# New queue orders and engine choices ahead of the first gate groups of a transformer block

## The chip, the cores and the metric

The kernel runs on one core of a Trainium2 chip. What is measured is the device time in microseconds. A core has five engines, each with an instruction queue that is worked off in order: TensorE (PE, with its weight loads shown apart as PEld), VectorE (DVE), ScalarE (ACT), GpSimd (POOL) and SyncE (SP), which here only issues DMA transfers. An instruction that must wait for a semaphore holds up all that stands behind it on its engine.

## What is computed

One block of a transformer in bfloat16, with 2048 rows (S) and width 448 (D): linear attention with 16 heads of 28 over feature maps, and a gated MLP of width 1792 (F).

```
x  = A_x                                      # 1 x 2048 x 448
q, k, v = split(layernorm(x) @ wqkv)          # 16 heads of 28
phi(t) = concat(softmax(t @ w_phi), softmax(-t @ w_phi))
kv = sum over s of phi(k)[s] v[s];   z = sum over s of phi(k)[s]
o  = (phi(q) @ kv) / (phi(q) . z + 1e-6)
h  = x + o @ wo
g, u = layernorm(h) @ w_gate, layernorm(h) @ w_up
out = h + (sigmoid(g) * u) @ w_down
```

## The kernel before

The rows are cut into 16 tiles of 128 rows, t = 0 to 15. The program builds a graph of about a thousand named operations with their data dependences; class `Graph` (L19 on) keeps them. Nothing orders them at run time but the table `ORDER` (from L209), which lists for each of the five queues the names in the order in which they are issued. Where an operation may run on one of two or three engines, its tuple of engines is given with it, and it goes to the engine in whose list its name stands (`Graph.op`). `emit` sets a semaphore wait wherever an operation needs another engine's result, or would overwrite what another still reads. So a name's place in the lists decides both the engine and the time.

The names, in order of the work:

- Loads on SP: `x0`, `x1` (one tile each), `x2`, `x4` ... `x14` (two tiles each); `ld_k0`, `ld_k2`, `ld_v0`, `ld_v2` (weights of k and v), `ld_q0` to `ld_q3` (weights of q, by transposing DMA), `ld_wo*`, `ld_wg*`, `ld_wu*`, `ld_wd0` to `ld_wd6` (output, gate, up and down weights). `wphi*` are small loads that ACT issues.
- First layernorm of tile t: `bst` and `agg` (mean and variance, DVE, L499 and L500), `ve1` (adds epsilon, L507), `pow1` (power -0.5, POOL only, L512), `nm1` (minus the mean, L510), `nb1` (bias, POOL only, L516), then `xn` (the normalized tile, L525 on ACT, L528 on DVE or POOL). `ve1`, `pow1`, `nm1`, `nb1` come by groups: tiles 0, 1, 2, 3 alone, then 4 and 5, 6 and 7, 8 to 11, 12 to 15; the number in the name is the first tile. Tiles 0 and 1 need no `nb1`; every other `xn` waits for the `nb1` of its group, whatever its engine.
- `xT`: transposes the normalized tile; for t < 4 on PE, with a copy `xTe` out of PSUM on ACT or DVE (`evac`, L485), else by a transposing DMA on SP (L538).
- Folding the feature map into the weights of k: `wT` (PE) and `wTe` (copy), `w2m0` (PE, L567) and `w2e0` (copy); `w2m1` and `w2e1` for q.
- k and v of a tile: `pp` and `vv` for pairs of the tiles 0 to 3, `pva`/`pvb` for the others (PE); `v1` copies v; `ek` takes two exponentials (ACT, L614 and L615), `ss` sums them (DVE, L618), `rs` inverts the sums (DVE, L619), `phi` multiplies (POOL or DVE, L622). `kva`/`kvb` add the tile to the running k/v sum in PSUM banks 6 and 7. There are 3 buffers for `phi`, 5 for `ek` and 5 for `v1`.
- `kvzones`, `kvzA` to `kvzD`: the masked copy of the k/v sum, with a column of ones (L426 to L429, L683, L687). They wait for `kvb15`.
- q by chunks of four tiles: `pqa`/`pqb` (PE), `eq` (two exponentials, ACT, L652 and L653).
- Attention output of a tile: `num` (PE), `rsm`, `qq`, `b`, `c`, `den`, `rden` (DVE, L714 to L725), `o` (POOL or DVE, L729), `oT` (transposed), `woa`/`wob` (PE).
- Residual and second layernorm: `h` (ACT for tiles 0 and 1, L748, else DVE, L751), `nm`, `sq` (ACT, L756), `ve` and `pow2` (POOL, L759 and L761), `hn` (DVE, L765), `hT`.
- MLP: gate groups `ga`/`gb` with tile and column group (PE), `sig` (ACT, L824), `hh` (DVE, L825), `dn`/`dp`/`dm`/`dl` (down projection, PE), `fin` (DVE), `out` (store).

`warm` are matmuls on zeros. Nearly all matmuls are recorded on line 296, that of the helper `both`, which issues two half-height matmuls side by side.

Of the kernel before, what the change touches and what calls it, by code (L numbers as in the profile page):

```python
# [925 lines left out]
```

## Time and profile before

| what | us |
|---|---|
| median of 3 runs | 205.27 (205.26 to 205.29) |
| span of the profiled execution, first to last instruction | 203.7 |
| busy PE | 196.7 (97%) |
| busy DVE | 135.9 (67%) |
| busy ACT | 97.4 (48%) |
| busy POOL | 57.9 (28%) |
| first gate matmul starts | 61.0 |

The span is that of one profiled execution; the time of a run lies 1.6 us above it. Busy matmul time is not time at full rate, as matmuls are pipelined. A row of the timeline gives start, length, engine, line, operation, the names of what it writes and reads, and in brackets the idle time before it with what ended it; rows of one kind that follow each other are merged (x3).

### The profile page before, as it was taken

How to read it: one execution, taken by the hardware profiler on the slowest of the kernel's cores; microseconds unless marked ns; L12 is line 12 of the kernel's file. 1: busy time of each engine (PE TensorE's matmuls, PEld its weight loads, DVE VectorE, ACT ScalarE, POOL GpSimd, SP SyncE). 2: the span in 40 equal slices, each digit the busy share in tenths (PEclk: the TensorE clock that was granted, in tenths of full speed). 3: DMA queues.
4: the chain of work that ended last, by engine and by line, in shares of the span. 5: the costliest groups of instructions: out<-in, count | busy, mean ns of one | idle time of the engine just before them, and what ended most of it. 6: DMA issues, size and time to landing. Idle time of an engine off the chain costs nothing.

```text
span 203.7 us, 5834 instructions
## 1 busy us (share of the span) xinstructions
PE 196.7 (97%) x2474; PEld 111.6 (55%) x2474; DVE 135.9 (67%) x340; ACT 97.4 (48%) x195; POOL 57.9 (28%) x98
## 2 busy tenths in 40 slices
...
GB/s 163 306 139 122 77 73 66 282 295 352 141 52 55 55 100 27 55 81 0 3 0 80 119 30 28 2 77 24 56 36 60 3 0 3 0 0 138 0 0 90
DMA packets 32866, 16.25 MB, mean 80 GB/s; under 512 B 25096, under 2 KB 31944, under 8 KB 32840
## 3 DMA queue, kind: packets, MB, share of 16 engines
...
q8 instruction: 19, 0.31, 0.7%
q10 hardware_dynamic: 504, 0.03, 0.2%
...
## 4 chain that ended last, share of the span: by engine, by line
PE 89%; DVE 4%; ACT 3%; DMA 1%; issue 1%; POOL 0%; DVEq 0%
PE psum L296 82%; PE psum L852 5%; DVE st L499 2%; DMA x_sb<-in_A_x_dram 1%; ACT eq L653 1%; ACT eq L652 1%; PE psum L567 1%; ACT junk L756 1%; ACT x_sb L748 1%; PE psum L492 1%; DVE kvz L683 1%; DVE mv L500 0%; DVE b_sb L717 0%; DVE c_sb L720 0%; POOL rst L512 0%
## 5 line engine op out<-in xcount | busy, mean ns | idle before, releaser
L296 PE MATMUL psum<-xnT,wg_sb 64*128 64x512 bf16 (+1 forms) x490 | 93.3, 333 | 0.4 <-ACT eq L653 0.2
L296 PE MATMUL psum<-xnT,wu_sb 64*128 64x512 bf16 (+1 forms) x490 | 93.0, 333 | 0.0
L824 ACT ACTIVATE sg_sb<-psum 128x512 bf16<-128x512 f32 (+1 forms) x70 | 35.0, 512 | 89.6 <-PE psum L296 89.0
L825 DVE SCALAR_TENSOR_TENSOR hhT<-sg_sb,psum 128x512 bf16<-128x512 bf16 (+1 forms) x70 | 39.0, 577 | 52.5 <-ACT sg_sb L824 52.1
L296 PEld LDWEIGHTS psum<-xnT,wg_sb 64*128 64x128 bf16 x490 | 44.3, 94 | 22.9 <-DVE hhT L825 4.8
L296 PEld LDWEIGHTS psum<-xnT,wu_sb 64*128 64x128 bf16 x490 | 44.3, 94 | 13.0
L296 PE MATMUL psum<-wd_sb,hhT 64*128 64x448 bf16 x336 | 36.9, 349 | 0.0
L296 PEld LDWEIGHTS psum<-wd_sb,hhT 64*128 64x128 bf16 x336 | 17.3, 94 | 14.8 <-DVE x_sb L751 0.6
L622 POOL TENSOR_TENSOR phi<-hhT,rs 128x896 bf16<-128x896 bf16 x14 | 24.1, 1738 | 0.9 <-PE psum L296 0.8
L296 PE MATMUL psum<-Wk,xnT 64*128 64x448 bf16 x112 | 22.3, 350 | 0.2
L296 PE MATMUL psum<-wv_sb,xnT 64*128 64x448 bf16 x112 | 22.4, 351 | 0.1
L759 POOL TENSOR_SCALAR ve<-ssq 128x1 f32<-128x1 f32 x16 | 3.1, 192 | 66.1 <-ACT junk L756 65.7
L618 DVE TENSOR_REDUCE ss<-hhT 128x32 f32<-128x896 bf16 x16 | 17.0, 1062 | 0.7 <-ACT hhT L615 0.7
L296 PE MATMUL psum<-xnT,Wq 64*120 64x512 bf16 x112 | 15.0, 385 | 0.1
L729 POOL TENSOR_TENSOR o_pad<-c_sb,rden 128x448 bf16<-128x448 bf16 x10 | 9.3, 936 | 15.6 <-DVE rden L725 13.4
L296 PE MATMUL psum<-wo_o,oT 64*128 64x448 bf16 x56 | 13.2, 350 | 0.0
L296 PE MATMUL psum<-wo_e,oT 64*128 64x448 bf16 x56 | 13.1, 349 | 0.0
L756 ACT ACTIVATE junk<-x_sb,nm 128x448 bf16<-128x448 bf16 x16 | 10.6, 661 | 1.9 <-DVE nm L754 1.8
L852 PE MATMUL psum<-wd_sb,hhT 128*128 128x448 bf16 (+2 forms) x70 | 11.1, 316 | 0.0
L859 DVE SCALAR_TENSOR_TENSOR x_sb<-psum,x_sb 128x448 bf16<-128x448 f32 (+2 forms) x17 | 9.4, 591 | 2.1 <-PE psum L852 1.6
L499 DVE BATCH_NORM_STATS2 st<-x_sb 128x6 f32<-128x448 bf16 x16 | 9.4, 611 | 1.9 <-DMA x_sb<-in_A_x_dram 1.9
L296 PEld LDWEIGHTS psum<-Wk,xnT 64*128 64x128 bf16 x112 | 7.6, 94 | 5.3 <-ACT hhT L615 0.7
...
## 6 DMA issues: line engine op xcount, KB each, us to landing
...
```

The costliest lines, as they stand in the source:

```text
L296: p = e.matmul(o, lhsT=w, rhs=r, start=st, stop=sp, tile_position=(row, 0))
L492: p = e.transpose(ps[:, kt * P:(kt + 1) * P], src, ident[:])
L499: op("dve", "bst%d" % t, lambda e: e.bn_stats(st1[:, t, :], x_sb[:, t, :]), r=[("x", t)], w=[("st1", t)])
L618: op("dve", "ss%d" % t, lambda e: e.tensor_reduce(ss[:, s, :], eks, AX.X, ALU.add), r=[("ek", s)], w=[("ss", s)])
L622: return e.tensor_tensor(phi[:, sp, :, :, :].rearrange("p b a n -> p (b a) n")[:, :, 0:56].rearrange("p b (h d) -> p b h d", h=2), eks.rea ...
L729: return e.tensor_tensor(o_pad[:, t % NO, off:off + D].rearrange("p (h d) -> p h d", h=H), c_sb[:, t % NS, :, 0:DH], rden[:, t % NS, :][:, ...
L756: op("act", "sq%d" % t, lambda e: e.activation(junk[:, t % 2, :], h_sb[:, t, :], ACT.Square, bias=nm2[:, t:t + 1], accum_out=ssq2[:, t:t + ...
L759: op("pool", "ve%d" % t, lambda e: e.tensor_scalar(ve2[:, t:t + 1], ssq2[:, t:t + 1], 1.0 / D, EPS, op0=ALU.mult, op1=ALU.add), r=[("ssq2" ...
L824: op("act", "sig" + nm, lambda e: e.activation(sg_sb[:, k, 0:N], bk(bg)[:, 0:N], ACT.Tanh, scale=0.5), r=[B(bg)], w=[("sg", k)])
L825: op("dve", "hh" + nm, lambda e: e.scalar_tensor_tensor(out=hhT[(t0 // 4) % NHH][:, ff, ns], in0=sg_sb[:, k, 0:N], scalar=1.0, in1=bk(bu)[ ...
L852: p = e.matmul(bk(b)[:, lo:hi], lhsT=hb[:, ff, TS(t)], rhs=wd_sb[:, ff, lo:hi], start=ff == 0, stop=ff == FT - 1)
L859: op("dve", "fin%d%s" % (t, nm), lambda e: e.scalar_tensor_tensor(out=h_sb[:, t, lo:hi], in0=bk(b)[:, lo:hi], scalar=0.5, in1=h_sb[:, t, l ...
```

## The change

Only the table `ORDER` changes; what each operation does, its buffers and its dependences stay. All five lists are new up to about the operations of the first gate group (tiles 0 and 1) and the same behind it. 38 operations change their engine:

- from ACT to DVE: `wTe0`, `wTe1`, `wTe2`, `xT0e`, `xT1e`, `xn4`, `xn13`, `xn15`, `w2e1_3`, `kvzones`
- from ACT to POOL: `xn6`, `xn11`, `xn14`
- from DVE to ACT: `wTe3`, `xT2e`, `v1_9`, `v1_10`; from POOL to ACT: `xn2`
- from DVE to POOL: `ve1_1`, `nm1_0`, `xn0`, `xn1`, `nm1_6`, `nm1_8`, `ve1_12`
- from POOL to DVE: `nm1_1`, `nm1_2`, `nm1_3`, `nm1_4`, `nm1_12`, `ve1_0`, `ve1_2`, `ve1_3`, `ve1_4`, `ve1_6`, `ve1_8`, `o2`, `o6`, `o7`

```diff
     "sp": (
-        "x1 x0 ld_k0 x2 ld_k2 x4 x6 ld_v0 x10 ld_v2 x8 ld_q2 ld_q1 ld_q0 x12 ld_q3 xT4 xT5 x14 xT6 xT7 xT8 xT9 xT10 "
-        "xT11 xT12 xT13 xT14 xT15 ld_wg0 ld_wu1 ld_wu3 ld_wd1 ld_wg1 ld_woe0 ld_wu0 ld_woe1 ld_woo0 ld_woo1 ld_wg3 "
-        "ld_wg2 ld_wd6 ld_wd2 ld_wd3 ld_wd5 ld_wd0 ld_wu2 oT2 oT3 oT5 oT4 oT6 oT7 ld_wd4 hT3 hT2 oT8 oT9 hT4 hT5 hT6 "
...
+        "x1 x0 x2 ld_k0 ld_k2 x4 x6 x10 ld_v2 x8 ld_v0 ld_wd4 ld_q2 x12 ld_q3 ld_q0 x14 ld_q1 xT4 ld_wg1 xT6 xT5 "
+        "xT7 xT8 xT9 xT10 xT11 ld_wg2 ld_wu3 xT12 ld_woo1 xT13 ld_wu0 xT14 xT15 ld_wu1 ld_woe0 ld_woe1 ld_wd2 "
+        "ld_wd0 ld_wg0 ld_wd5 ld_wu2 ld_wg3 ld_woo0 oT2 oT3 oT5 ld_wd1 oT4 oT6 oT7 hT3 ld_wd3 hT2 ld_wd6 oT8 oT9 "
...
     ),
     "act": (
-        "wphi3 wphi2 wphi1 wphi0 wTe0 wTe1 xT1e xT0e wTe2 w2e0_0 w2e0_1 w2e0_2 w2e0_3 xn3 xn4 ek0 ek1 xn5 v1_0 v1_1 "
-        "xn6 ek2 v1_2 v1_3 ek3 w2e1_1 ek4 v1_4 ek5 v1_5 w2e1_0 v1_6 ek6 xn11 ek7 v1_7 xn12 ek8 xn13 ek9 w2e1_3 w2e1_2 "
-        "ek10 xn14 ek11 xn15 v1_11 ek12 eq0_0 ek13 v1_13 ek14 v1_14 ek15 kvzones v1_15 eq0_1 kvzB eq1_0 eq1_1 eq2_0 "
-        "oT0e eq2_1 h1 h0 sq1 sq0 eq3_0 eq3_1 sig0_1 sig0_0 sig0_3 sig0_2 sig0_5 sig0_4 sq2 sig0_7 sig0_6 sq3 sig0_9 "
-        "sig0_8 sq5 sig0_11 sig0_10 sig0_13 sig0_12 sig2_1 sig2_0 sq4 sig2_3 sig2_2 sq7 sq6 sig2_5 sig2_4 sig2_6 "
...
+        "wphi0 wphi2 wphi1 wphi3 w2e0_0 wTe3 w2e0_1 w2e0_2 w2e0_3 xn2 xn3 xT2e ek0 ek1 v1_0 v1_1 xn5 ek2 v1_2 v1_3 "
+        "ek3 w2e1_0 ek4 v1_4 v1_5 ek5 w2e1_1 v1_6 ek6 ek7 v1_7 ek8 xn12 ek9 v1_9 w2e1_2 ek10 v1_10 ek11 v1_11 ek12 "
+        "eq0_0 ek13 v1_13 ek14 v1_14 ek15 v1_15 eq0_1 kvzB eq1_0 eq1_1 eq2_0 oT0e eq2_1 h1 h0 sq1 sq0 eq3_0 eq3_1 "
+        "sig0_1 sig0_0 sig0_3 sig0_2 sig0_5 sig0_4 sig0_7 sig0_6 sq2 sq3 sig0_9 sig0_8 sig0_11 sig0_10 sig0_13 "
+        "sig0_12 sq5 sig2_1 sig2_0 sq4 sig2_3 sig2_2 sq7 sq6 sig2_5 sig2_4 sig2_6 sig2_7 sig2_8 sig2_9 sig2_10 "
...
     ),
     "pe": (
-        "warm0 warm1 warm2 wT0 wT1 xT1 warm3 xT0 warm4 warm5 wT2 w2m0_0 wT3 warm6 w2m0_1 w2m0_2 warm7 w2m0_3 warm8 "
-        "ppa0 warm9 ppb0 vva0 xT3 xT2 vvb0 ppa2 ppb2 vva2 vvb2 w2m1_1 w2m1_0 kva0 pva4 kvb0 pvb4 pva5 kva1 pvb5 kvb1 "
-        "pva6 kva2 pvb6 pva7 w2m1_2 w2m1_3 pvb7 pva8 kvb2 kva3 pvb8 kvb3 pva9 kva4 pvb9 kvb4 pva10 kva5 pvb10 pva11 "
-        "kvb5 kva6 pvb11 pqa0_0 pva12 kvb6 kva7 pvb12 kvb7 pqb0_0 kva8 pva13 kvb8 kva9 pvb13 pva14 kvb9 kva10 pvb14 "
-        "kvb10 kva11 pva15 kvb11 pvb15 kva12 pqa0_1 kvb12 pqb0_1 kva13 pqa1_0 kvb13 kva14 pqb1_0 kvb14 kva15 kvb15 "
-        "pqa1_1 num0 num1 pqb1_1 pqa2_0 pqb2_0 num2 pqa2_1 oT0 pqb2_1 oT1 num3 woa0 wob0 num4 pqa3_0 pqb3_0 pqa3_1 "
-        "num5 pqb3_1 hT1 hT0 num6 ga0_1 ga0_0 gb0_1 gb0_0 woa2 num7 ga0_3 ga0_2 gb0_3 gb0_2 wob2 ga0_5 ga0_4 gb0_5 "
-        "gb0_4 num8 woa4 ga0_7 ga0_6 gb0_7 gb0_6 wob4 num9 ga0_9 ga0_8 gb0_9 gb0_8 woa6 ga0_11 ga0_10 gb0_11 gb0_10 "
-        "wob6 ga0_13 ga0_12 gb0_13 gb0_12 dn0_0 dn0_4 ga2_1 ga2_0 gb2_1 gb2_0 dn0_8 dn0_11 ga2_3 ga2_2 gb2_3 num10 "
...
+        "warm0 warm1 warm2 warm3 warm4 warm5 wT1 wT0 xT1 wT2 w2m0_0 wT3 xT0 w2m0_1 warm6 w2m0_2 warm7 w2m0_3 warm8 "
+        "warm9 ppa0 xT2 ppb0 vva0 xT3 vvb0 ppa2 vva2 ppb2 vvb2 kva0 w2m1_0 kvb0 w2m1_1 pva4 pvb4 pva5 w2m1_2 pvb5 "
+        "kva1 pva6 kvb1 kva2 pvb6 pva7 w2m1_3 pvb7 pva8 kvb2 kva3 pvb8 kvb3 pva9 kva4 pvb9 pva10 kvb4 kva5 pvb10 "
+        "kvb5 pva11 pqa0_0 pvb11 kva6 pva12 kvb6 kva7 pvb12 kvb7 pqb0_0 pva13 kva8 pvb13 kvb8 pva14 kva9 pvb14 "
+        "kvb9 pva15 kva10 pvb15 kvb10 kva11 pqa0_1 kvb11 kva12 pqa1_0 kvb12 pqb0_1 kva13 pqb1_0 kvb13 kva14 kvb14 "
+        "kva15 kvb15 pqa1_1 num0 pqb1_1 num1 pqa2_0 num2 pqb2_0 pqa2_1 oT0 pqb2_1 oT1 num3 woa0 wob0 num4 pqa3_0 "
+        "pqa3_1 pqb3_0 num5 pqb3_1 hT1 hT0 num6 ga0_1 ga0_0 gb0_1 gb0_0 woa2 num7 ga0_3 ga0_2 gb0_3 gb0_2 wob2 "
+        "ga0_5 ga0_4 gb0_5 gb0_4 num8 woa4 ga0_7 ga0_6 gb0_7 gb0_6 wob4 ga0_9 ga0_8 gb0_9 gb0_8 woa6 ga0_11 ga0_10 "
+        "gb0_11 gb0_10 wob6 num9 ga0_13 ga0_12 gb0_13 gb0_12 dn0_0 dn0_4 ga2_1 ga2_0 gb2_1 gb2_0 dn0_8 dn0_11 "
...
     ),
     "dve": (
-        "zero bd0 bst1 agg1 ve1_1 bst0 agg0 nm1_0 xn1 xn0 bst2 agg2 bst3 agg3 bst4 bst5 wTe3 agg4 agg5 bst6 bst11 "
-        "bst10 agg11 bst9 bst7 agg6 agg7 agg9 bst8 agg8 agg10 xT3e xT2e ss0 nm1_8 nm1_6 rs0 ss1 bst13 rs1 bst12 ss2 "
-        "bst14 rs2 agg14 xn8 ss3 agg13 agg12 rs3 xn9 bst15 ss4 agg15 xn10 ve1_12 ss5 rs4 ss6 rs5 ss7 rs6 v1_8 ss8 "
-        "v1_9 rs7 ss9 rs8 v1_10 ss10 rs9 rs10 ss11 v1_12 rs11 phi10 ss12 rs12 ss13 rs13 ss14 rs14 ss15 rs15 phi15 "
-        "kvzA kvzD kvzC rsm0 qq0 b0 rsm1 c0 qq1 den0 b1 rden0 c1 rsm2 den1 qq2 rden1 b2 c2 den2 oT1e rsm3 qq3 b3 c3 "
-        "den3 rden2 rden3 rsm4 nm1 qq4 b4 nm0 c4 den4 rden4 hn1 rsm5 qq5 b5 hn0 c5 hT1e den5 hT0e rden5 rsm6 qq6 b6 "
-        "c6 den6 hh0_1 hh0_0 rsm7 rden6 qq7 b7 c7 hh0_3 den7 hh0_2 h2 rden7 nm2 h3 hh0_5 rsm8 hh0_4 qq8 b8 c8 nm3 "
-        "den8 hh0_7 hh0_6 h5 h4 rsm9 hn3 hh0_9 hh0_8 rden8 nm5 qq9 hn2 nm4 hh0_11 hh0_10 h7 h6 o8 hh0_13 hh0_12 b9 c9 "
-        "den9 rden9 o9 hh2_1 hh2_0 hh2_3 rsm10 hh2_2 hn4 qq10 nm7 b10 nm6 c10 hn5 hh2_5 hh2_4 hn6 fin0 fin1 hn7 hh2_6 "
...
+        "zero bd0 bst1 agg1 bst0 nm1_1 agg0 bst3 ve1_0 bst2 agg3 agg2 wTe1 wTe0 ve1_3 xT1e wTe2 nm1_3 ve1_2 nm1_2 "
+        "xT0e bst4 bst5 agg4 bst6 agg5 bst7 nm1_4 agg6 agg7 bst8 ve1_4 ve1_6 bst11 bst9 xn4 xT3e ss0 agg11 agg9 "
+        "rs0 ss1 bst13 bst10 agg8 agg10 rs1 ve1_8 bst14 ss2 xn8 rs2 ss3 xn10 agg13 xn9 rs3 bst12 bst15 ss4 agg12 "
+        "agg14 agg15 rs4 ss5 ss6 nm1_12 rs5 rs6 v1_8 ss7 ss8 rs7 w2e1_3 xn13 ss9 xn15 rs8 ss10 rs9 ss11 v1_12 rs10 "
+        "rs11 ss12 phi10 rs12 ss13 rs13 ss14 rs14 ss15 rs15 phi15 kvzones kvzD kvzC kvzA rsm0 qq0 b0 rsm1 c0 qq1 "
+        "den0 b1 rden0 c1 rsm2 den1 qq2 rden1 b2 c2 den2 oT1e rsm3 qq3 b3 c3 den3 rsm4 rden2 qq4 nm1 b4 nm0 c4 "
+        "rden3 den4 o2 rsm5 hn1 qq5 b5 hn0 c5 hT1e den5 hT0e rden5 rsm6 qq6 b6 c6 rden4 den6 hh0_1 hh0_0 rsm7 qq7 "
+        "b7 c7 hh0_3 den7 hh0_2 rden6 h3 h2 o6 hh0_5 hh0_4 rsm8 rden7 qq8 o7 nm3 b8 hh0_7 nm2 hh0_6 h5 h4 hh0_9 "
+        "hh0_8 hn3 c8 hn2 den8 rden8 hh0_11 hh0_10 h6 h7 o8 rsm9 hh0_13 hh0_12 qq9 nm5 b9 nm4 c9 den9 rden9 o9 "
...
     ),
     "pool": (
-        "neghalf ident0 ident phipad wqpad mask0 nm1_1 pow1_1 ve1_0 pow1_0 nm1_2 mask1 ve1_2 ve1_3 pow1_3 nm1_3 "
-        "pow1_2 nb1_3 ve1_4 nm1_4 pow1_4 nb1_4 nb1_2 xn2 mask2 opad0 ve1_6 pow1_6 ve1_8 v1ones pow1_8 nb1_6 phi0 "
-        "nb1_8 xn7 phi1 phi2 phi3 nm1_12 pow1_12 nb1_12 phi4 phi5 phi6 phi7 phi8 phi9 phi11 phi12 phi13 phi14 o0 o1 "
-        "o2 o3 ve1 pow2_1 ve0 pow2_0 o5 o4 o6 o7 ve2 pow2_2 ve3 pow2_3 ve5 ve4 pow2_4 pow2_5 ve7 pow2_7 ve6 pow2_6 "
-        "ve8 ve9 o11 pow2_9 o12 pow2_8 ve10 pow2_10 ve11 pow2_11 ve12 pow2_12 ve14 pow2_14 ve15 ve13 pow2_15 pow2_13 "
+        "ident0 neghalf phipad ident ve1_1 pow1_1 nm1_0 xn1 pow1_0 xn0 pow1_2 pow1_3 nb1_2 wqpad mask0 v1ones "
+        "nb1_3 pow1_4 nb1_4 pow1_6 mask1 opad0 nm1_6 nb1_6 xn6 phi0 xn7 nm1_8 pow1_8 nb1_8 phi1 phi2 phi3 xn11 "
+        "ve1_12 pow1_12 phi4 nb1_12 phi5 xn14 phi6 phi7 phi8 phi9 mask2 phi11 phi12 phi13 phi14 o0 o1 ve1 pow2_1 "
+        "ve0 pow2_0 o3 o5 o4 ve2 ve3 pow2_3 pow2_2 ve4 ve5 pow2_4 pow2_5 ve7 pow2_7 ve6 pow2_6 ve8 ve9 o11 pow2_9 "
+        "o12 pow2_8 ve10 pow2_10 ve11 pow2_11 ve12 pow2_12 ve14 pow2_14 ve15 ve13 pow2_15 pow2_13 "
```

## The prediction

> **What bounds the kernel now.** I read the busy times by stretch first, then the chain that ended last, then the queue of the engine that feeds it. The first view gives the busy time of each engine in stretches cut where the work changes (columns: stretch, its length, then PE, PEld, DVE, ACT, POOL).
>
> ```profile
> 12.00:15.50 3.50, 3.40 (x36) 1.43 (x32) 3.41 (x13) 3.38 (x8) 3.35 (x10) 1.00 0.58 105
> 15.50:18.20 2.70, 2.60 (x34) 1.12 (x31) 2.70 (x5) 2.44 (x6) 2.70 (x5) 1.00 0.59 127
> 18.20:43.20 25.00, 25.00 (x432) 14.87 (x428) 23.53 (x44) 24.13 (x51) 23.78 (x16) 1.00 0.61 139
> ...
> 61.00:203.70 142.70, 140.17 (x1628) 79.70 (x1628) 82.14 (x209) 44.48 (x98) 15.58 (x34) 1.00 0.19 40
> ```
>
> From the first gate group (61.0 us) on, TensorE is busy 140.2 of 142.7 us, and the change leaves its order alone there but for one early step. So the time is decided by when that group can start. Before it lies the k/v stage (18 to 43 us), where four engines are all nearly full: PE 25.0, ACT 24.1, POOL 23.8, DVE 23.5 of 25. None of them can be given work for nothing. The chain shows what closes the stage (start, length, what):
>
> ```profile
> 24.48 18.74 PE psum L296 x336
> 43.22 0.01 issue
> 43.23 1.25 PE psum L296 x30
> 44.49 0.05 issue
> 44.53 0.31 PE psum L296 x8
> 44.84 0.02 issue
> 44.86 0.39 DVE kvz L683
> ```
>
> kvb15, the last piece of the k/v sum, ends at 44.84; only then can the masked copies kvz and num0 (46.20) follow. What kvb15 waits for are the phi tiles: 14 of 16 are POOL's. The timeline of POOL (start, length) from phi0 to phi14:
>
> ```profile
> 15.53 1.70 POOL L622 TENSOR_TENSOR phi<-hhT,rs 128x896 bf16<-128x896 bf16 x1
> 17.19 0.20 POOL L516 TENSOR_TENSOR nb<-nm,rst 128x4 f32<-128x4 f32 x1
> 17.37 0.77 POOL L528 TENSOR_SCALAR xn_pad<-x_sb,nm,rst 128x512 bf16<-128x512 bf16 x1
> 18.11 5.25 POOL L622 TENSOR_TENSOR phi<-hhT,rs 128x896 bf16<-128x896 bf16 x3
> 23.49 0.33 POOL L510 TENSOR_SCALAR nm<-mv 128x4 f32<-128x4 f32 x1
> 23.86 1.04 POOL L512 TENSOR_TENSOR rst<-ve,neghalf 128x4 f32<-128x4 f32 x1
> 25.05 0.20 POOL L516 TENSOR_TENSOR nb<-nm,rst 128x4 f32<-128x4 f32 x1
> 25.20 8.42 POOL L622 TENSOR_TENSOR phi<-hhT,rs 128x896 bf16<-128x896 bf16 x5
> 34.00 1.70 POOL L622 TENSOR_TENSOR phi<-hhT,rs 128x896 bf16<-128x896 bf16 x1 [0.39 <-PE psum L296]
> 36.11 7.06 POOL L622 TENSOR_TENSOR phi<-hhT,rs 128x896 bf16<-128x896 bf16 x4 [0.41 <-PE psum L296]
> ```
>
> phi14 ends at 36.11 + 7.06 = 43.17. In these 27.6 us POOL idled 0.8. The queue is as full as TensorE's, and today it finishes only just before it would decide: phi15 on DVE ends at 42.74 + 1.38 = 44.12 and kva15, kvb15 take 0.72 more; after phi14 four pieces would be left (24 matmuls took 0.79, so 32 take 1.05, with 0.18 for the wait between halves about 1.25), giving 44.4. The slack of POOL is 0.4 us plus its 0.8 of idle.
>
> **Part 1, POOL's queue behind phi0 (decides, +2.3).** The new order puts there: the 14 phi (24.1 by the rows), xn7, xn11, xn14 (3 x 0.77), nm1_8, pow1_8, nb1_8 and ve1_12, pow1_12, nb1_12 (the trio above went from 23.49 to 25.20, 1.71; the second with 0.24 for ve instead of 0.33), and mask2 (0.33, from the row of its kind). That is 24.1 + 2.3 + 3.3 + 0.3 = 30.0 us, against 26.8 of work before; xn11, xn14, mask2, pow1_8 and nm1_8 or ve1_12 are what came in, nm1_12 went to DVE. The 0.8 of idle is swallowed first. The phi wait for nothing else in that stretch: rs1 to rs3 come out of DVE at about 18.1, 20.6, 22.7 and are asked for at 20.0, 21.7, 23.4.
>
> **When phi0 starts (+0.3).** I followed the new front by hand, each step by the duration of its row. agg1 ends at 3.71 as now. ve1_1 (0.25), pow1_1 (0.57), nm1_0 (0.24), xn1 (0.77 on POOL, 0.41 on DVE before), pow1_0, xn0 take POOL to 7.27; today xn0 is done at 6.25. On DVE bst3 waits for x2, now the third load (issued 1.70 instead of 2.17, landing about 4.9); then bst2, agg3, agg2, wTe1, wTe0 end at 7.2, so w2m0_0 runs at 7.2 as it does now, and xT0 gets through TensorE at 7.85 to 8.2. w2e0_3 ends at 10.0 (10.12 now), ppa0 starts at 10.1 (10.18), ek0 at 12.0 (12.12): the entry to the stage gains nothing beyond 0.1. Behind xT0e DVE has five bst (0.55 apart), four agg (0.12), nm1_4, so ve1_4 is ready at 8.2 + 0.35 + 2.75 + 0.5 + 0.1 = 11.9. POOL stands at pow1_4 until then; what is queued behind it: nb1_4, pow1_6 (0.72 each pow), mask1 0.33, opad0 0.36, nm1_6 0.24, nb1_6 0.2, xn6 0.77, and so phi0 at 15.8 (15.53 now). The same wait holds xn4 on DVE (it needs nb1_4, 13.0), and behind xn4 xT3e and ss0; rs0 would be ready at 15.45. Bounds: phi0 can't start before ek0's end + ss0 + rs0 = 12.95 + 1.05 + 0.35 = 14.35; three waits of 0.35 (the largest gap in DVE's front is 0.57) give 16.8. I take 15.8.
>
> **Sum of the stage.** phi14 ends at 15.8 + 30.0 = 45.8, kvb15 at 45.8 + 0.05 + 1.25 = 47.1 against 44.84: +2.3. TensorE's own path doesn't decide: pva4 goes from 18.2 to 18.8, since kva0 waits for phi0 (17.5) and kvb0, w2m1_1 now stand ahead of it; but the projections stand earlier among the kv pieces, so pvb15 comes near 40 as now. ACT loses six xn (0.71 apart), w2e1_3 and kvzones (0.5 each) and gains xn2, v1_9 and v1_10 (0.42 each): some 3.7 us less. That is hidden, since ACT ends waiting for kvb15 (0.78 already now). xn12 on ACT and xn13 on DVE must wait for nb1_12 (about 29.3, 25.25 now); the cover of that is the same 3.7 us.
>
> **Port.** Three phi with three xn of DVE beside them (19.71, 21.39, 23.33) took 5.25, 1.75 each; five without took 8.42, 1.68 each: 0.07 for each xn beside, and six stand there now, so 0.2 at most on POOL, inside the rounding of 30.0. [...]
>
> **Part 2, kvz to the gates (0).** kvzones (0.27 + 0.46 on ACT) goes to DVE between phi15 and kvzD; DVE waits there 0.74 now and longer then. num1 behind pqb1_1 is ready 0.4 us before rsm1 (47.70) asks. num2 ahead of pqb2_0 pushes eq2_0 by some 0.15, and ACT has 0.95 of idle before h1. o2 on DVE (0.62, by the row of o8 at 76.70) delays hn1 by 0.45 and hn0 by 0.1; hT1 waits for pqb3_1 anyway (58.45), and ga0_1 for eq3_1 (60.96). If ACT's cover were gone, this would cost 0.1 to 0.45. Bulk loads now stand between the xT on SP (0.45 to 0.6 of issue each); pva5 needs xT5 at 20.2, it lands near 19.5. A loss of up to 0.5 there would be eaten by POOL's lateness.
>
> **Part 3, first gate groups (+0.4).** o6 and o7 (0.62 each, 0.94 on POOL) enter DVE, which is full from 62 to 74 (1.97 of 2.00 us at 72 to 74). rden6 leaves the way of hh0_3, where TensorE stalls now (65.45 to 65.94): gain 0.05. hn3 comes 0.8 later than 72.23, o7 near 69.6 instead of 68.0, so oT7 lands 72.1 to 72.7 for woa6 at 72.1: 0 to 0.6. On SP ld_wd3 stands between hT3 and hT2, so hT2 goes from 74.0 to 75.2 and lands (2.4 to 4.2) at 77.6 to 79.4 for ga2_1 at 78.4: 0 to 1.0; wd3 itself (3.0 for such a load) at 77.7 for dn0_4 at 77.7. num9 moves behind wob6 and meets den8 (75.0). Bounds -0.2 and +1.5; I take 0.4, nearer the low end, since TensorE's arrival is the later one in most of the cases. Afterwards TensorE has no idle time to win it back.
>
> Sum: 203.7 + 2.3 + 0.4 = 206.4 of span; the median (205.27) lies 1.57 above the profiled span, so **208.0**.
>
> **Rivals.**
> The queue stays, but phi0 starts at its earliest (14.35): the stage loses 45.8 - 1.45, so 0.9, and the gates nothing: 206.2. For it: DVE's wait for x2 is an estimate. Against: xn6 stands ahead of phi0 and needs pow1_6. Chance 0.10.
> Faster: ACT set the pace. It is full from 12 to 42 us (waits 0.16 and 0.55), and 3.7 us leave it; the order lets pvb15 pass three kv pieces (0.25 each), so ek15, phi15 and num0 come 0.75 earlier: 204.5. It decides only if phi14 ends by 42.4, that is if POOL's 30.0 us took 26.6, a phi 1.48 instead of 1.72. No row of 14 is so short. Chance 0.12.
> Slower yet: DVE and POOL hold each other up (POOL at pow1_4, DVE at xn4) so that phi0 comes at 16.8, and the gates pay 1.4: 205.27 + 3.3 + 1.4 = 210.0. Chance 0.12.
> The forecast itself has 0.66, with 207.0 to 209.2 as its own range.
>
> **How the numbers follow.** Slower holds the forecast, the first rival and the third, less 0.03 at their edge: 0.85; faster 0.11 and same 0.04 come from the second. What is under 0.2% (0.4 us) counts as same here. The range 206.0 to 209.9 takes in the first rival and all but the top of the third, and leaves out the faster case.
>
> **What would show it.** POOL without idle from phi0 to phi14, phi0 at 15.8, phi14's end near 45.8; kvb15 released by POOL and not by DVE; TensorE waiting for POOL at the kv pieces of the last tiles; num0 near 48.5 and ga0_1 near 63.3; from there a length of 142.7 to 143.7. It is wrong if phi14 ends before 43.2, or if phi of the new run are shorter than 1.6, or if POOL shows idle there again: then the queue isn't the bound.

## The result, and the profile after

The changed kernel takes **212.96 us** (median of four runs, 212.06 to 214.17) against 205.28 (205.26 to 205.55) on the same chip: 1.0374 times as long, with a 95% interval of 1.0334 to 1.0414. It is slower by 7.7 us, where the forecast had it slower by 2.7. (The lists of the change name 39 operations, not 38.) The profiled execution of it took 214.17 with a span of 212.4; all line numbers from 296 on are higher by 2 (both is L298, phi L624, xn L530, rs L621, kvz L685).

Read first where the time lies. The busy times by stretch, in the columns of the prediction and with the granted clock behind them, cut at kvz and at the first gate matmul of the new run:

```profile
15.50:18.20 2.70, 2.58 (x34) 1.28 (x32) 2.70 (x8) 1.81 (x4) 2.70 (x3) 1.00 0.78 169
18.20:43.20 25.00, 21.39 (x339) 11.53 (x338) 24.95 (x40) 18.90 (x39) 21.66 (x20) 1.00 0.64 140
43.20:50.20 7.00, 6.53 (x138) 4.13 (x136) 6.48 (x12) 4.52 (x9) 5.01 (x3) 1.00 1.05 312
50.20:67.07 16.87, 13.62 (x217) 7.49 (x214) 14.74 (x47) 15.00 (x23) 4.83 (x8) 0.99 0.12 26
67.07:212.40 145.33, 141.96 (x1628) 80.68 (x1628) 83.55 (x212) 44.60 (x98) 13.85 (x32) 0.99 0.20 43
```

The k/v stage ends at kvz at 50.17 instead of 44.86 (+5.3). From there to the first gate matmul it is 16.90 instead of 16.15 (+0.75), and from there to the end 145.3 instead of 142.7 (+2.6). In the row of the k/v stage TensorE, ACT and POOL have all become idler (21.4, 18.9 and 21.7 of 25, where they had 25.0, 24.1 and 23.8). Only VectorE is busier: 24.95 of 25.00. An instruction that stands still after it was issued counts as busy here, as will be seen; so 24.95 is not all work. The bound of the stage has moved to an engine that the prediction had at 23.5. The chain that ended last, in order of time, says the same: from 20 us to kvz it is almost all VectorE.

```profile
19.99 1.76 DVE xn_pad L530
21.75 0.26 DVE rs L621
22.01 0.94 DVE ss L620
22.95 0.98 DVE xn_pad L530
...
40.89 2.24 DVE phi L624
43.13 0.26 DVE rs L621
...
47.42 2.02 DVE phi L624
...
49.48 0.31 PE psum L298 x8
...
49.84 0.31 PE psum L298 x8
...
50.17 0.40 DVE kvz L685
```

An xn of 1.76 us is strange: the same instruction takes 0.37 four us later. To see why, two timelines have to be laid beside each other. POOL first:

```profile
15.96 1.70 POOL L624 TENSOR_TENSOR phi<-hhT,rs 128x896 bf16<-128x896 bf16 x1
...
19.90 1.70 POOL L624 TENSOR_TENSOR phi<-hhT,rs 128x896 bf16<-128x896 bf16 x1
22.09 1.70 POOL L624 TENSOR_TENSOR phi<-hhT,rs 128x896 bf16<-128x896 bf16 x1 [0.49 <-DVE rs L621]
24.66 1.70 POOL L624 TENSOR_TENSOR phi<-hhT,rs 128x896 bf16<-128x896 bf16 x1 [0.88 <-DVE rs L621]
...
28.52 1.70 POOL L624 TENSOR_TENSOR phi<-hhT,rs 128x896 bf16<-128x896 bf16 x1
...
36.88 3.35 POOL L624 TENSOR_TENSOR phi<-hhT,rs 128x896 bf16<-128x896 bf16 x2 [0.49 <-DVE rs L621]
...
40.48 1.70 POOL L624 TENSOR_TENSOR phi<-hhT,rs 128x896 bf16<-128x896 bf16 x1
43.47 5.01 POOL L624 TENSOR_TENSOR phi<-hhT,rs 128x896 bf16<-128x896 bf16 x3 [1.29 <-DVE rs L621]
```

And VectorE's rows from the same timeline:

```profile
19.99 1.76 DVE L530 TENSOR_SCALAR xn_pad<-x_sb,nm,rst 128x512 bf16<-128x512 bf16 x1
21.67 0.34 DVE L621 RECIPROCAL rs<-ss 128x32 f32<-128x32 f32 x1
...
22.88 1.06 DVE L530 TENSOR_SCALAR xn_pad<-x_sb,nm,rst 128x512 bf16<-128x512 bf16 x1
...
23.95 0.37 DVE L530 TENSOR_SCALAR xn_pad<-x_sb,nm,rst 128x512 bf16<-128x512 bf16 x1
24.24 0.34 DVE L621 RECIPROCAL rs<-ss 128x32 f32<-128x32 f32 x1
...
28.89 1.35 DVE L512 TENSOR_SCALAR nm<-mv 128x4 f32<-128x4 f32 x1
...
33.83 1.00 DVE L530 TENSOR_SCALAR xn_pad<-x_sb,nm,rst 128x512 bf16<-128x512 bf16 x1
...
40.81 2.32 DVE L624 TENSOR_TENSOR phi<-hhT,rs 128x896 bf16<-128x896 bf16 x1
43.05 0.34 DVE L621 RECIPROCAL rs<-ss 128x32 f32<-128x32 f32 x1
...
47.42 2.00 DVE L624 TENSOR_TENSOR phi<-hhT,rs 128x896 bf16<-128x896 bf16 x1
```

Compare ends, not starts. phi1 on POOL ends at 21.60; xn8, begun under it at 19.99, ends at 21.75. phi2 ends at 23.79, xn10 at 23.94. phi4 ends at 30.22, the tiny nm1_12 (4 numbers a partition) at 30.24. phi11 ends at 42.18, phi10 on VectorE at 43.13, which is 0.95 later; where it met no phi of POOL, in the run b_dve_order below, it took 1.02. By these ends VectorE's instruction does not run slowly: it **stands until POOL's phi is over** and then runs. Then comes the second half of the loop. rs2 stands behind xn8 in VectorE's queue, ends at 22.01, and phi2 starts at 22.09 after 0.49 of idle; rs3 stands behind xn10 and xn9, and phi3 idles 0.88. VectorE waits for phi(t), and then POOL waits for the rs of phi(t+1): a lockstep. The 0.49 is the sum of its steps: xn8 ends 0.15 after phi1, rs2 0.26 after that, and phi2 starts 0.08 later. POOL's idle from phi0 to phi14 is 3.15 us, all of it waiting for rs; it was 0.8, waiting for TensorE. (Waits under 0.2 us are left out here and below.)

For the tail, two pairs of rows from the busy times by stretch: the last 3 us ahead of the first gate matmul and the 3 us behind it, first in the changed kernel,

```profile
64.00:67.07 3.07, 1.18 (x25) 0.75 (x26) 3.03 (x9) 2.56 (x3) 1.39 (x3) 0.96 0.40 80
67.07:70.00 2.93, 2.93 (x28) 2.41 (x30) 1.76 (x6) 0.36 (x1) 1.78 (x2) 0.50 0.31 56
```

and in the kernel before:

```profile
58.00:61.01 3.01, 1.65 (x30) 0.82 (x27) 2.93 (x11) 2.97 (x4) 0.58 (x2) 1.00 0.22 44
61.01:64.00 2.99, 2.99 (x62) 2.68 (x64) 2.71 (x9) 0.71 (x2) 1.74 (x2) 1.00 0.27 49
```

TensorE was busy 55% of the stretch ahead of the gates, now 38%; and behind it the granted clock is 0.50 for 3 us, in which 28 matmuls are recorded instead of 62, though TensorE counts as busy all through both (2.93 and 2.99 us). In the chain the 52 matmuls from the first gate matmul on take 4.25 us (67.07 to 71.31) instead of 2.71, so the half clock costs 1.5 us. It is not in every run: the two of the changed kernel with a mean clock of 0.992 took 214.17 and 213.55, the two with 1.0 took 212.37 and 212.06. The rest of the tail is in the chain:

```profile
62.45 1.04 POOL rst L763
...
63.51 0.41 DVE hn_pad L767
...
64.68 0.77 DVE hn_pad L767
...
82.25 0.25 SPq L774
82.50 0.04 issue
82.55 3.70 DMA wd_sb<-in_B_w_down_dram
```

pow2_1 on POOL (rst, L763) takes 1.04 instead of the usual 0.55 beside o2 on VectorE (62.44 to 63.06), and hn0 takes 0.85 instead of 0.4 behind POOL's o4 (64.36 to 65.30), 0.15 after which it ends: one engine holds up the other again, now on the way to the gates. And ld_wd3, which the new order puts between hT3 and hT2, is issued so late that TensorE waits 0.8 us for it.

### The profile page after: what moved, and what is told of

It is laid out like the page before. It is cut to its first block, busy times and chain, and to the rows that moved or that the text cites. A ratio compares the mean times of both kernels' runs of the same rounds, so it can differ in the third digit from the quotient of the medians.

```text
span 212.4 us, 5838 instructions
## 1 busy us (share of the span) xinstructions
PE 199.1 (94%) x2474; PEld 112.6 (53%) x2474; DVE 144.1 (68%) x355; ACT 93.1 (44%) x185; POOL 57.0 (27%) x93
## 3 DMA queue, kind: packets, MB, share of 16 engines
HBM read 8.34 MB, written 1.84 MB: 48 GB/s over the span
## 4 chain that ended last, share of the span: by engine, by line
PE 66%; DVE 20%; DMA 4%; POOL 4%; issue 2%; ACT 2%; SPq 1%; POOLq 0%
PE psum L298 60%; DVE ss L620 5%; PE psum L854 5%; DMA wk_sb<-in_A_wqkv_dram 2%; DVE xn_pad L530 2%; DVE phi L624 2%; DVE rs L621 2%; DMA wd_sb<-in_B_w_down_dram 2%; DVE st L501 2%; POOL rst L514 1%; DVE c_sb L722 1%; ACT junk L758 1%; DVE b_sb L719 1%; DVE hn_pad L767 1%; POOL phi L624 1%
## 5 line engine op out<-in xcount | busy, mean ns | idle before, releaser
L298 PE MATMUL psum<-xnT,wg_sb 64*128 64x512 bf16 (+1 forms) x490 | 94.7, 338 | 0.4 <-DVE rden L727 0.2
L298 PE MATMUL psum<-xnT,wu_sb 64*128 64x512 bf16 (+1 forms) x490 | 94.4, 338 | 0.0
L298 PEld LDWEIGHTS psum<-xnT,wg_sb 64*128 64x128 bf16 x490 | 45.0, 95 | 23.1 <-DVE hhT L827 4.9
L298 PEld LDWEIGHTS psum<-xnT,wu_sb 64*128 64x128 bf16 x490 | 45.0, 95 | 13.1
L298 PE MATMUL psum<-wd_sb,hhT 64*128 64x448 bf16 x336 | 37.1, 349 | 0.8 <-DMA wd_sb<-in_B_w_down_dram 0.8
L298 PEld LDWEIGHTS psum<-wd_sb,hhT 64*128 64x128 bf16 x336 | 17.4, 94 | 15.8 <-DMA wd_sb<-in_B_w_down_dram 1.2
L624 POOL TENSOR_TENSOR phi<-hhT,rs 128x896 bf16<-128x896 bf16 x14 | 23.6, 1701 | 3.2 <-DVE rs L621 3.1
L298 PE MATMUL psum<-Wk,xnT 64*128 64x448 bf16 x112 | 22.4, 350 | 1.8 <-ACT hhT L617 1.6
L298 PE MATMUL psum<-wv_sb,xnT 64*128 64x448 bf16 x112 | 22.5, 351 | 0.1
L620 DVE TENSOR_REDUCE ss<-hhT 128x32 f32<-128x896 bf16 x16 | 16.5, 1043 | 0.0
L298 PE MATMUL psum<-xnT,Wq 64*120 64x512 bf16 x112 | 14.5, 383 | 0.0
L298 PE MATMUL psum<-wo_e,oT 64*128 64x448 bf16 x56 | 13.3, 351 | 0.1
L298 PE MATMUL psum<-wo_o,oT 64*128 64x448 bf16 x56 | 13.3, 352 | 0.0
L298 PEld LDWEIGHTS psum<-Wk,xnT 64*128 64x128 bf16 x112 | 7.6, 94 | 6.8 <-ACT hhT L617 2.3
L298 PEld LDWEIGHTS psum<-v,phi 64*128 64x128 bf16 x256 | 6.9, 94 | 7.8 <-POOL phi L624 3.3
L616 ACT ACTIVATE hhT<-psum 128x448 bf16<-128x448 f32 x16 | 8.8, 550 | 4.7 <-PE psum L298 4.6
```

The lines of the kernel that those rows point to most:

```text
L298: p = e.matmul(o, lhsT=w, rhs=r, start=st, stop=sp, tile_position=(row, 0))
L616: e.activation(ek[:, s, :, 0, :], src, ACT.Exp)
L620: op("dve", "ss%d" % t, lambda e: e.tensor_reduce(ss[:, s, :], eks, AX.X, ALU.add), r=[("ek", s)], w=[("ss", s)])
L624: return e.tensor_tensor(phi[:, sp, :, :, :].rearrange("p b a n -> p (b a) n")[:, :, 0:56].rearrange("p b (h d) -> p b h d", h=2), eks.rea ...
```

## The experiments

The letters in the expectations are theories: L, the lockstep above; Q, POOL's longer queue alone is the cost; D, the bulk loads that now stand between the xT on SP bring the tiles late. Where an expectation gives no letter, it says its theory in words. All edits are moves within the lists of names, except the two marked. A ratio is to runs of the kernel before taken beside the run (medians 205.28 to 205.48). The table has what the readings rest on (us; "idle" is POOL's between phi0 and phi14; kvz is its start).

| run | phi0 | idle | phi14 ends | kvz | time (lowest to highest) |
|---|---|---|---|---|---|
| before | 15.53 | 0.8 | 43.17 | 44.86 | 205.28 |
| after | 15.96 | 3.15 | 48.48 | 50.17 | 212.96 (212.06 to 214.17) |
| b_pool_queue | 15.60 | 0.0 | 44.60 | 46.28 | 206.84 (206.49 to 207.0) |
| b_dve_xn | 15.64 | 1.3 | 43.77 | 45.47 | 205.97 (205.75 to 207.63) |
| b_dve_order | 15.46 | 4.3 | 45.48 | 47.17 | 207.96 (207.69 to 208.1) |
| b_dve_and_pool | 15.45 | 2.1 | 45.71 | 47.41 | 207.95 (207.74 to 208.65) |
| a1_nm12_pool | 15.42 | 3.15 | 47.87 | 49.56 | 212.64 (211.43 to 214.21) |
| a5_xn13_xn15_act | 15.18 | 1.7 | 46.99 | 48.68 | 212.77 (211.07 to 212.93) |
| a9_no_dve_xn | 15.80 | 1.2 | 47.03 | 48.71 | 211.61 (210.75 to 212.82) |
| as_phi_halves | 15.83 | 0.5 | 49.16 | 50.37 | 215.18 (213.61 to 215.68) |
| a4_wd_early | 15.57 | 3.15 | 48.08 | 49.77 | 212.82 (211.85 to 213.44) |
| a8_old_tail | 15.32 | 3.15 | 47.84 | 49.52 | 210.46 (210.09 to 210.67) |
| a10_no_dve_xn_old_tail | 15.46 | 1.1 | 46.40 | 48.09 | 208.83 (208.35 to 209.24) |

phi0 itself comes up to 0.9 us earlier or later in kernels whose front is the same, and takes kvz with it. So the length from phi0 to phi14's end says more of the stage than kvz alone: it is 27.6 before, and 32.5 in the changed kernel, in a4 and in a8, where nothing of the stage differs.

### One part of the change put into the kernel before

**POOL's longer queue alone** (b_pool_queue):

```diff
 "pool"
-phi3 nm1_12 pow1_12 nb1_12 phi4 phi5 phi6
+phi3 xn11 nm1_12 pow1_12 nb1_12 phi4 phi5 xn14 phi6
...
-phi9 phi11
+phi9 mask2 phi11
```

(xn11 and xn14 leave ACT's list, and mask2 leaves its place ahead of phi0.)

> The kernel before with xn11 and xn14 on POOL instead of ACT and mask2 behind phi9: 1.87 us more on POOL behind phi0 and nothing else. Theory Q (what I forecast of the queue): the 0.8 of idle is swallowed, phi14's end 1.1 to 1.9 later than 43.17, then phi15 waits for it, so kvz 1.1 to 1.9 later than 44.86, and 206.4 to 207.2. If POOL's queue has more slack than that: 205.3 to 206.

206.84, 1.0067 times before [1.0050, 1.0084]; 1.87 us of work came in and took about 2.2, above all because mask2 met VectorE's phi10 and took 1.18 instead of 0.33; the 0.8 of idle was swallowed, and phi14 and kvz come 1.42 later. So the way in which the prediction priced the queue is right, but for what its instructions meet there.

**Two xn on VectorE** (b_dve_xn: xn13 behind rs7 and xn15 behind ss9 on VectorE instead of ACT):

> The kernel before with xn13 and xn15 alone moved from ACT to DVE (behind rs7 and ss9). Theory L: beside a running phi each takes until its end plus 0.15, up to 1.8 instead of 0.38, so DVE gets 0.8 to 3.2 us more in a stage where it idles 1.5 of 25: kvz 0.3 to 1.7 later than 44.86, time 205.6 to 207.0. Without such a wait: 0.6 us of work for DVE, 1.4 less for ACT, kvz within 0.3 and 205.1 to 205.6.

205.97, 1.0030 [1.0011, 1.0049]. xn13 fell on a boundary between two phi and took 0.31; xn15 took 0.79 and ended 0.15 after phi7; rs8 stood behind it, and POOL idled 0.49 ahead of phi8, the lockstep in small. Whether an xn pays depends on where it falls.

**VectorE's order alone** (b_dve_order):

```diff
 "dve"
-ss2 bst14 rs2 agg14 xn8 ss3 agg13 agg12 rs3 xn9 bst15 ss4 agg15 xn10 ve1_12 ss5 rs4 ss6 rs5
+ss2 bst14 xn8 rs2 agg14 ss3 xn10 agg13 agg12 xn9 rs3 bst15 ss4 agg15 ve1_12 ss5 rs4 ss6 nm1_12 rs5
...
-rs7 ss9 rs8
+rs7 xn13 ss9 xn15 rs8
```

(xn13 and xn15 leave ACT's list, nm1_12 leaves POOL's.)

> The kernel before with the VectorE part of the change alone: xn13 and xn15 on VectorE, nm1_12 on VectorE behind ss6, xn8 ahead of rs2, xn10 and xn9 ahead of rs3. POOL's queue gets 0.33 shorter. Lockstep: xn8, xn10, nm1_12 stand for a phi each (1.0 to 1.8 us), POOL idles 2.5 to 3.5 us behind phi0 instead of 0.8, kvz +1.4 to +2.4, time 206.7 to 207.9. Rival (it needs POOL's longer queue to hurt): kvz +0.3 to +0.8 as with xn13 and xn15 alone, time 205.6 to 206.2.

207.96, 1.0121 [1.0100, 1.0142], kvz +2.31, though POOL has less to do than before. POOL's timeline in this run:

```profile
20.22 1.70 POOL L622 TENSOR_TENSOR phi<-hhT,rs 128x896 bf16<-128x896 bf16 x1 [0.49 <-DVE rs L619]
22.87 1.70 POOL L622 TENSOR_TENSOR phi<-hhT,rs 128x896 bf16<-128x896 bf16 x1 [0.94 <-DVE rs L619]
24.67 1.01 POOL L512 TENSOR_TENSOR rst<-ve,neghalf 128x4 f32<-128x4 f32 x1
26.93 0.20 POOL L516 TENSOR_TENSOR nb<-nm,rst 128x4 f32<-128x4 f32 x1 [1.25 <-DVE nm L510]
...
34.28 3.44 POOL L622 TENSOR_TENSOR phi<-hhT,rs 128x896 bf16<-128x896 bf16 x2 [0.49 <-DVE rs L619]
38.82 6.66 POOL L622 TENSOR_TENSOR phi<-hhT,rs 128x896 bf16<-128x896 bf16 x4 [1.10 <-DVE phi L622]
```

The waits of the changed kernel ahead of phi2 and phi3 (0.49 and 0.88 there, 0.49 and 0.94 here) come up again, at the same places, in a kernel in which nothing else was changed. nm1_12, moved to VectorE, is late in another way: nb1_12 waits 1.25 for it. So of the 4.3 us of idle 1.9 is for rs, 1.25 for nm1_12 and 1.10 ahead of phi11. The rival (harmless without the longer queue) is out.

**Both** (b_dve_and_pool, the two diffs together):

> The VectorE part as in the run before and POOL's longer queue (xn11 and xn14 on POOL, mask2 behind phi9), nothing else of the change. Lockstep: the two add up, since POOL is the bound in both: 1.4 from the queue and 1.4 to 2.4 from the waits, kvz +2.8 to +3.8, time 208.1 to 209.3. Rival (the waits hide in the longer queue): about the longer queue alone, 206.7 to 207.3.

207.95, 1.0128 [1.0102, 1.0154]: no more than VectorE's order alone. Between the two theories: xn11 runs in time that POOL would have idled (nb1_12 now waits 0.64 instead of 1.25), so idle fell by 2.1 while work rose by 1.9 (and mask2, behind phi9, met VectorE's phi10 and took 1.17). Terms that end in the same wait do not add up. kvz is at +2.55 of the changed kernel's +5.3.

### Parts of the change undone

**nm1_12 back to POOL** (a1_nm12_pool: behind ve1_12 in POOL's list):

> The changed kernel with one small instruction moved: nm1_12 (128x4 values, 0.15 us of work) from DVE back to POOL. Theory L (lock): DVE's nm1_12 took 1.36 us only because POOL's phi4 was running (it ended 0.02 us after phi4); with it gone DVE's rs6 and all behind it come up to 1.2 us earlier, kvb15 by 0.5 to 1.2, and the time falls from 212.96 to 211.8 to 212.5. Theory Q (POOL's own queue decides): POOL gets 0.3 us more, so 213.0 to 213.3.

212.64, 1.0357 [1.0305, 1.0409]: no difference that these runs can tell. Its 1.35 is gone, but xn15 first waited 0.96 for a transposing DMA, then met the next phi and took 1.40; the four waits of POOL for rs (0.49, 0.88, 0.49, 1.29) are the same to 0.01 us.

**xn13 and xn15 off VectorE too** (a5_xn13_xn15_act: a1 and):

```diff
 "act"
-ek8 xn12 ek9 v1_9 w2e1_2 ek10 v1_10 ek11 v1_11
+ek8 xn12 ek9 xn13 v1_9 w2e1_2 ek10 v1_10 ek11 xn15 v1_11
 "dve"
-w2e1_3 xn13 ss9 xn15 rs8
+w2e1_3 ss9 rs8
```

> The changed kernel with nm1_12 on POOL, and xn13 and xn15 back on ACT behind ek9 and ek11 (late enough that their buffers are free). In the run before this, taking nm1_12's wait away alone left the kvz copies 0.6 earlier only, since xn15 then waited 0.96 for a transposing DMA and 1.0 more for a phi. Theory L (DVE is the bound of the k/v stage, made long by waits for POOL's phi and by xn that stand in its queue): DVE loses 3.1 us of the 5.8 it waited, kvz starts 2.0 to 3.0 earlier than 50.17, and the time is 210.0 to 211.3. Theory Q (POOL's own queue): POOL has the same 30 us, so kvz within 0.5 of 50.17 and 212.5 to 213.3.

kvz is 1.5 earlier than in the changed kernel, idle 1.7 instead of 3.15. But 0.8 of the 1.5 is phi0, which came at 15.18; from phi0 to phi14's end it is 31.8 instead of 32.5. The time (212.77, 1.0331 [1.0289, 1.0372]) shows little of it: three of the four runs had a mean clock of 0.992, and the one with 1.0 took 211.07.

**All five xn off VectorE** (a9_no_dve_xn: a5 with xn8 behind w2e1_0, xn10 and xn9 behind ek4 on ACT):

> The changed order with nm1_12 on POOL and all five xn of the k/v stage on ACT (xn8 behind w2e1_0, xn10 and xn9 behind ek4, xn13 behind ek9, xn15 behind ek11), so that VectorE has no xn beside a phi. Lockstep (VectorE waits for the phi beside its xn, POOL then waits for the late rs): POOL idles under 0.8 us from phi0 to phi14, phi14 ends 30.0 to 30.5 after phi0 (31.8 with xn13 and xn15 alone off VectorE), kvz near 47.1, time 210.8 to 211.6. Rival (the waits on VectorE are idle that would be there anyway, the length of the stage comes from elsewhere): kvz stays at 48.5 or later, time 212.3 or more.

211.61, 1.0296 [1.0241, 1.0350], at the upper edge of what was expected; kvz, at 48.71, lies where the rival had it. Every wait of POOL for rs is gone, and phi9 ends 22.4 after phi0 (24.3 in the changed kernel). But phi11 then waits 1.19 us for TensorE, which still has to read the buffer that phi11 overwrites, and now meets VectorE's phi10, takes 2.39 instead of 1.70, and phi14 ends 31.2 after phi0. The 3.15 of idle that went, less these 1.19 and 0.69, is the 1.3 that was won. So the waits for rs are not idle that would be there anyway, but most of what their end wins is lost again at the stage's next limits: of the 4.9 us by which the change lengthens the stage from phi0 on, this run gives back 1.3. The run with the old tail shows the same, here in POOL's timeline:

```profile
19.39 5.01 POOL L622 TENSOR_TENSOR phi<-hhT,rs 128x896 bf16<-128x896 bf16 x3
24.39 0.77 POOL L528 TENSOR_SCALAR xn_pad<-x_sb,nm,rst 128x512 bf16<-128x512 bf16 x1
...
30.99 6.67 POOL L622 TENSOR_TENSOR phi<-hhT,rs 128x896 bf16<-128x896 bf16 x4
37.61 0.33 POOL L418 TENSOR_SCALAR_AFFINE_SELECT maskK<-maskK 128x116 f32<-128x116 f32 x1
39.04 7.36 POOL L622 TENSOR_TENSOR phi<-hhT,rs 128x896 bf16<-128x896 bf16 x4 [1.11 <-PE psum L296]
```

phi1 to phi3 are one row of 5.01 us now, where the changed kernel shows three rows with 0.49 and 0.88 between them.

**rs ahead of xn** (a6_rs_first: a5 with rs2 ahead of xn8 and rs3 ahead of xn10 and xn9):

> The kernel of the run with nm1_12 on POOL and xn13, xn15 on ACT, and on DVE rs2 put ahead of xn8, rs3 ahead of xn10 and xn9. Theory L: xn8 and xn10 still stand behind phi1 and phi2, but the rs that the next phi needs no longer stand behind them, so POOL's idle time of 0.49 and 0.88 ahead of phi2 and phi3 goes; kvz starts 0.8 to 1.4 earlier than the 48.68 of that run, time 210.6 to 211.8 against its 212.77. If POOL's idle time there has another cause (TensorE's loop), it stays and kvz is within 0.3 of 48.68.

212.44, 1.0344 [1.0330, 1.0359], and the gain of 0.8 to 1.4 in kvz did not come: 48.67 as in a5. The idle ahead of phi2 and phi3 is gone, but xn9 now met phi3 and stood 1.69, and POOL stood 1.19 for the buffer of xn11 and 0.55 for the statistics that ve1_12 reads, so that phi4 started at 28.12 in both. The order on one queue only chooses who pays.

**Two that went wrong by placement.** a2_xn_act was a1 with xn8, xn10, xn9 as in a9, xn13 behind xn12 and xn15 behind v1_9 on ACT; a3_pool_less the changed kernel with xn11 (behind ek4) and xn14 (behind ek9) on ACT and mask2 ahead of phi0.

> The changed kernel with nm1_12 on POOL and xn8, xn9, xn10, xn13, xn15 on ACT instead of DVE. Theory L: six DVE instructions that stood 4.3 us in all behind a running phi are gone, and 1.6 us of DVE work with them; DVE stops being the bound, and POOL's queue (30 us from phi0 at 16.0) is next, phi14's end near 46.2 instead of 48.5, kvb15 near 47.5 instead of 50.1: 209.8 to 211. Theory Q: no change beyond 0.3, 213.

> The changed kernel with 1.5 us taken off POOL behind phi0 (xn11 and xn14 to ACT) and mask2 (0.33) put ahead of phi0. Theory Q: phi14 and with it the time come 1.5 to 1.9 earlier, 211.1 to 211.5. Theory L: POOL already idles 3.2 us waiting for DVE's rs behind phi0, so it only idles more: 212.5 to 213.3.

215.95 (1.0516 [1.0488, 1.0544]) and 215.5 (1.0478 [1.0448, 1.0507]): both slower than the change. In a2 ACT stood 3.1 us at an xn whose buffer (one of three) a transposing DMA had not yet read, in a3 2.7 us, and all exponentials stood behind it. They say little of L or Q, but this: an instruction that may have to wait must not stand on the queue that feeds everybody. In a2 POOL's idle ahead of phi2 and phi3 was gone nevertheless, which led to a9.

### Other causes

**The bulk loads on SP** (a7_loads_late: a1 with ld_wu0, ld_woo1, ld_wu3, ld_wg2, ld_wg1 behind xT15):

> The changed kernel with nm1_12 on POOL, and the five loads of gate, up and output weights that stand between the transposes on SP (ld_wg1, ld_wg2, ld_wu3, ld_woo1, ld_wu0) put behind xT15, as they were before. Theory D (the transposes land late behind these loads and hold up TensorE and the xn buffers): xT12 lands 1.0 to 1.5 earlier, xn15's wait of 0.96 for it goes, kvz 0.7 to 1.0 earlier than the 49.56 of the run with nm1_12 alone, time 211.0 to 212.0. Theory L: xn15 starts earlier but meets the same phi and ends with it, kvz within 0.3 of 49.56, 212.3 to 212.8.

213.67, 1.0401 [1.0368, 1.0434], kvz 49.85: no gain, and from phi0 to phi14's end 32.46 us where a1 has 32.45. D is out.

**A shorter stand** (as_phi_halves: each phi on POOL issued as two instructions of half the columns):

> The changed kernel, same orders, with each of POOL's 14 phi cut in two instructions of half the width (POOL's o of 448 columns takes 0.94, so a phi 1.75 to 1.9 instead of 1.70). Theory L: a DVE instruction that meets a phi waits for the end of a half and not of the whole: xn8 takes at most 1.1 instead of 1.76, phi10 and phi15 at most 1.9, the 5.8 us of waiting on DVE fall by 2 to 3 us, kvz starts 1 to 2.5 earlier than 50.17 although POOL has 1 to 2 us more work. Theory Q: POOL's work grows, so kvz is 1 to 2 later.

215.18, 1.0441 [1.0395, 1.0488]. The stretches on VectorE fell as they would if VectorE stood until the end of the one instruction of POOL that it met: xn8 from 1.76 to 1.00, nm1_12 from 1.35 to 0.74, phi10 from 2.32 to 1.08, and POOL's idle to 0.5; no xn took more than 1.05. But two halves take 1.84 instead of 1.70, phi14 ends at 49.16, and kvz, which L had 1 to 2.5 earlier, is 0.2 later at 50.37. So the run settles that VectorE stands behind POOL's instruction; that a shorter stand brings the stage to its end sooner, it does not show.

**A fourth buffer for phi in the kernel before** (b_phi4, a changed constant):

> The kernel before with four buffers for phi instead of three. There POOL idles 0.39 and 0.41 ahead of phi9 and phi11 for a buffer that TensorE still reads, phi14 ends at 43.17, and phi15, issued on DVE at 42.74, takes 1.38 instead of 0.95 since it stands behind phi14 for 0.44. Theory L and Q together: without that idle phi14 ends 0.4 to 0.8 earlier, phi15 no longer meets it, kvz 0.2 to 0.45 earlier: 204.8 to 205.2. If TensorE alone sets the end of the stage: 205.3 to 205.5.

205.33, 0.9993 [0.9985, 1.0001]: POOL's idle of 0.8 is gone, but kvz comes only 0.15 earlier, less than the 0.2 to 0.45 expected, since phi11 now met VectorE's phi10 sooner and took 2.42 (2.09 before).

### The tail

**The last loads early** (a4_wd_early: ld_wd1, ld_wd3, ld_wd6 ahead of oT2):

> The changed kernel with ld_wd1, ld_wd3, ld_wd6 put ahead of oT2 on SP. The trace shows TensorE waiting for wd_sb until 86.25, a load that was issued behind hT3 at 82.25. Without that wait dn0_4 starts 0.8 to 1.2 earlier: 211.8 to 212.2 if TensorE is the bound from there on; no change if the gates after it wait for hT2 anyway.

212.82, 1.0372 [1.0345, 1.0398]. The wait for wd_sb left the chain, and a transfer of the transposed attention output (oT, 2.49), for which TensorE waits 0.6, took its place. The run with a mean clock of 1.0 took 211.85, the changed kernel's two 212.06 and 212.37: little or nothing is gained.

**The earlier kernel's orders behind the k/v sum** (a8_old_tail: all five lists of the kernel before from behind phi14, phi15 and kvb15 on, but for the kvz copies, which stay as changed, and the loads, which are as in a4), and the same with the xn of a9 (a10_no_dve_xn_old_tail):

> The changed orders up to phi14, phi15 and kvb15, and the orders of the kernel before from the kvz copies on (o2, o6, o7 back on POOL, ld_wd1, ld_wd3, ld_wd6 ahead of oT2). Theory L for the tail (o2 on DVE holds up POOL's pow2_1 by 0.48, POOL's o4 holds up hn0 by 0.44) and the late wd3: kvz stays near 50.2, from there to the first gate 16.1 as before instead of 16.9, and from the gate on 142.7 instead of 143.2 or more: time 210.2 to 211.2. If the tail costs nothing, as I forecast for it, 212 to 213.

> The run before with the earlier kernel's five orders behind the k/v sum (phi14 on POOL, phi15 on VectorE, kvb15 on TensorE), ld_wd1, ld_wd3, ld_wd6 ahead of oT2. Lockstep: what is left of the change is POOL's longer queue and the later phi0; kvz near 47.0 (+2.1), so 207.6 to 208.4, which is the forecast of the change. Rival: kvz 48.5 or later, 209.3 or more.

210.46 (1.0243 [1.0228, 1.0259]) and 208.83 (1.0164 [1.0139, 1.0190]). With the old tail the clock is 1.0 in all eight runs, kvz to the gate takes 16.2 again, and from the gate to the end 142.6 and 142.7, as before. So undoing the tail takes off 2.5 of the 7.7 us (in which there is a phi0 of 15.32 instead of 15.96; the profiles of the tail itself make it 0.7 up to the gates and 0.6 to 2.8 behind them), and taking the xn off VectorE 1.6 more (210.46 less 208.83; kvz 1.43 earlier). What is left in a10, 3.5 us, is by its profile POOL's longer queue, the 1.1 that phi11 waits for TensorE, and what phi10 and phi15 on VectorE cost beside POOL's phi; no run parts these. That run's kvz, 48.09, lies 1.0 above the forecast's 47.1. None of these kernels is faster than the one before.

## Why the prediction was wrong in size

**Right.** Slower, and in part through POOL's queue: phi0 was put at 15.8 and came at 15.96 (in kernels with the same front it came between 15.0 and 16.0, so part of that nearness is luck); work behind phi0 was put at 30.0 and measured 29.4; b_pool_queue confirms that such work, beyond the idle that it fills, delays kvz one for one. The wait for wd3 behind hT3 was named with its place. Its own sign of failure, "if POOL shows idle there again", came up and told where to look. Its sign that kvb15 would be released by POOL and not by VectorE did not: the chain has VectorE's phi15 (47.42 to 49.43) just ahead of the last pieces.

**The step that failed** is the one headed **Port**, with the sentence of Part 1, "The phi wait for nothing else in that stretch". It priced six xn beside phi at 0.2 us in all, by how much POOL's phi were stretched. (Five stand there; xn4 runs ahead of phi0. nm1_12, which is as exposed, was not counted.) POOL's rows were the wrong side to look at. In the trace of before, the three xn happened to start just ahead of the end of a phi (19.71 under a phi that ended at 19.81, 21.39 under 21.65), so both sides paid little. phi10 and phi15 on VectorE, 1.43 and 1.38 instead of 1.02, each ending 0.95 after a phi of POOL, showed that one of the two engines had stood, and I had read phi15's 1.38 as its duration; so did POOL's phi11, which took 2.09 beside phi10 and is hidden in the row of 7.06 for four. In the new order xn8, xn10, xn13, xn15, nm1_12, phi10 and phi15 together stand about 6.6 us (their rows less 0.37 for an xn, 0.15 for nm1_12 and 1.02 for a phi); and the rs stand behind them: rs2 and rs3, which I had ready at 20.6 and 22.7, end at 22.01 and 24.58. The cost: POOL's idle 3.15 instead of none in the forecast, and at the end 1.69 from phi14 to kvz instead of 1.3, since phi15 starts only when phi14 is over (in the halved run, where it need not, 1.21). With phi0's 0.16 and 0.6 of less work, that is the 3.0 us by which the stage missed. The sum says where the time went, not what would come back without the waits for rs: in a9 that was 1.3.

The rows agree with one another: in the changed kernel xn8, xn10, xn13 and xn15 end 0.14 to 0.15 after the phi of POOL that they met; there and in the kernel before, phi10 and phi15 on VectorE end 0.94 to 0.95 after theirs; and ss, a TENSOR_REDUCE, takes 1.02 to 1.09 in both, beside a phi or not. The prediction had priced the meeting on POOL, where its cost came up on VectorE and came back to POOL as waits for rs.

**Part 2 (0)** measured 0.75: by the chain, o2 on VectorE and o4 on POOL meet pow2_1 (1.04 instead of 0.55) and hn0 (0.85 instead of 0.4); I had counted o2's own 0.62 only. **Part 3 (+0.4)** measured 2.6 in the profiled run, of which 1.5 is the half clock. Where the clock held behind the gates, the same tail took 0.5 more than before in a1 and 2.2 more in a9, in which TensorE waits 1.1 us for oT and 0.8 for wd_sb: the size of this term differs from run to run with when these transfers land. a4 shows that ld_wd3 was only one of two waits ending close together. The clock was in no term: I had taken TensorE's hole ahead of the gates as idle that costs what it lasts.

The rival nearest to what happened was the third, where VectorE and POOL hold each other up; it had the two waiting for each other's results ahead of phi0, not VectorE held up by POOL's phi behind it, and ended at 210.0.

**Open.** How the 5.3 us of the stage split: b_dve_and_pool has 2.55 with phi0 unmoved; 0.4 are phi0, and nm1_8, pow1_8 and ve1_12 behind phi0 are 1.5 by their rows, which no run tried alone; that leaves some 0.8. Why phi0 came between 15.0 and 16.0 in kernels whose front was the same was not tried either.
